# Linear attention and a gated expert layer on one core: q's clamp, the gates and the slots' tags on GpSimd, and the first pick ahead of q's phi

## The chip, the cores and the metric

The kernel runs on one core of a Trainium2 chip. A core has TensorE (PE in the profile; its weight loads are PEld), VectorE (DVE), ScalarE (ACT), GpSimd (POOL) and SyncE (SP), each with an instruction queue that it works through in order, and 16 DMA engines that the queues of SP, ACT and POOL feed. The metric is the time of one execution in device microseconds (us), the median of several runs.

## The reference

Eight batches of 576 tokens. First a linear attention over 8 heads of width 64, then for each token one expert out of 8, with a locality rule: the first token takes the expert of its largest logit, a later token takes its own only if its local gate is below one half, and else it keeps the expert of the token before it.

```python
def phi(x):
    return np.where(x > 0, x, np.exp(x) - 1.0) + 1.0
q_p, k_p = (phi(q), phi(k))
kv = np.einsum('bhsd,bhse->bhde', k_p, v)
z = np.sum(k_p, axis=2)
num = np.einsum('bhsd,bhde->bhse', q_p, kv)
den = np.einsum('bhsd,bhd->bhs', q_p, z)[..., None] + 1e-06
x = num / den                       # then (8, 576, 512), heads side by side
...
logits = np.einsum('bsd,de->bse', x, w_gate)
local_gate = 1.0 / (1.0 + np.exp(-np.einsum('bsd,de->bse', x, w_local).squeeze(-1)))
...
            if s == 0 or local_gate[b, s] < 0.5:
                e = fresh_e
            else:
                e = prev_e if prev_e >= 0 else fresh_e
...
            p = np.exp(ls)
            p /= p.sum() + 1e-09
            h = np.maximum(x[b, s] @ w1[e], 0.0)
            out[b, s] = p[e] * (h @ w2[e])
```

Everything is float32; `w1` is 8 x 512 x 1024 and `w2` 8 x 1024 x 512.

## The kernel before

**The bet.** The kernel assumes that in each batch every token ends with the expert of token 0. It computes that expert's output for the whole batch, and beside it a table `bad` that counts the tokens for which the assumption fails (a local gate below one half and another best expert). At the end the count is summed, and only if it is above 0 does a slow general program run (line 697).

**Stages of a batch `a`.** q, k and v come in two halves of four heads (`n = 2a + j`), each load 576 KB on SP's queue into a few fixed slots (4 for k, 2 for q, 3 for v). For each half:

- `E`: ScalarE takes the exponential of k or q (L229); for k, and for the four q halves of the batches 0 and 1 (`both`), it also writes relu in place (L231).
- `P` (`phi`): VectorE combines the two. Where relu is there, one instruction, `min(e, 1) + r` (L238, L246). Where it is not, that is for q from half 4 on, two: `max(r + 1, 1)` in place (L248, the clamp), then `min(e, that)` (L249).
- `VC`: GpSimd (for half 1 ScalarE) copies v beside a column of ones (L257). `K`: TensorE multiplies k and v over the tokens (L266); `KC` copies the result out of psum.
- `Q`, `QL`: TensorE transposes q (L277, L290), ScalarE copies it out (`QC`, `QLC`). The last 64 tokens, token 0 among them, go separately and early: `QL`, `NL` (numerators), `DL` (division, L303 to L306), `XL` (transpose of x, L364), `XLC` (copy to `xT`, L368), `R 0` (logits of these tokens, L379), `RC 0`.
- `N`, `D`, `X`, `XC`, `R 1`: the same for the other 512 tokens (L318, L306, L352, L357, L385).
- `PK` (`pick`): VectorE finds token 0's expert, and whether one of three weight slots in SBUF holds it already. `BK` (`book`) then writes the slots' `tag` and `age` (L418 to L424).
- `W`: GpSimd issues the DMA of w1 and w2 (float32 in memory, bf16 in SBUF), for batch 0 straight into `wcur`, later into a slot and only on a miss (L444, L446). Ahead of the later ones stands a tiny copy, `seen` (L438), that waits for the weights of the batch before. `CW` (`use`): VectorE copies a slot into `wcur` (L456).
- `SB`, `SBC`: the expert's number is spread over 128 partitions.
- The gate: `S1` (VectorE: maximum and difference, L476, L478), `S2` (ScalarE: exponential, L481), `S3` (VectorE, fourteen instructions L486 to L509: which token differs, the count `bad`, the sum and the gate value `pr`).
- `H`, `HC`: hidden layer, eight tiles on TensorE (L517), relu on ScalarE (L524). `O`, `OC`: output, five tiles (L534, L538), scaled by `pr` on ScalarE (L548, L550). `ST`: the stores on SP.

**What sets the order.** The order on every engine is fixed by hand, by a small list planner (`in_order`): each step has an engine, an assumed length, a rank (the lower goes first) and a list of steps that it needs; the planner plays this through and emits the steps in the order of their start. `WL` is a step that stands for the landing of weights; it exists only in the planner. The waits on the chip come from the tiles: an instruction waits for the writers and readers of what it touches. So a need that isn't a touch of the same tile changes an order, and adds no wait. Attention runs two batches (`LEAD = 2`) ahead of the expert layer; psum has two buffers for attention (`a`) and two for the expert layer (`m`).

Of the kernel before, what the change touches and what calls it, by code (L numbers as in the profile page):

```python
# [79 lines left out]
def kernel(  # L80
# [11 lines left out]
    nc = tc.nc  # L92
# [31 lines left out]
    bad = keep.tile([P, B], F32, name="bad")  # L124
    flag_i = keep.tile([1, 1], I32, name="flag_i")

    with ExitStack() as main:
# [105 lines left out]
        def phi(n, x, both=False, c0=0, c1=C):  # L233
# [10 lines left out]
            if both:  # L244
                for g in range(2):
                    nc.vector.scalar_tensor_tensor(e[:, g], e[:, g], 1.0, r[:, g], Alu.min, Alu.add)  # L246
            else:
                nc.vector.tensor_scalar(r, r, 1.0, 1.0, Alu.add, Alu.max)  # L248
                nc.vector.tensor_tensor(e, e, r, op=Alu.min)  # L249

# [162 lines left out]
        def book(b):  # L413
# [4 lines left out]
            nc.vector.tensor_copy(sf, si[:, 0:1])  # L418
            at = sm_.tile([1, E], F32, name="at")
            nc.vector.tensor_scalar(at, iof[0:1], sf, None, Alu.is_equal)  # L420
            for row, to in ((tag, e0f), (age, 0.01 * (b + 1))):
                dif = sm_.tile([1, E], F32, name="dif")
                nc.vector.scalar_tensor_tensor(dif, row, to, at, Alu.subtract, Alu.mult)
                nc.vector.tensor_tensor(row, row, dif, op=Alu.subtract)  # L424
# [48 lines left out]
        def soft(b):  # L473
            lt = lt_all[:, b]
            mx = st[b, "mx"] = gp.tile([P, NC], F32, name="mx")
            nc.vector.tensor_reduce(mx, lt[:, :, :E], axis=AX.X, op=Alu.max)  # L476
            ex = st[b, "ex"] = gp.tile([P, NC, E], F32, name="ex")
            nc.vector.tensor_tensor(ex, lt[:, :, :E], bc(mx), op=Alu.subtract)  # L478

        def soft_exp(b):  # L480
            nc.scalar.activation(st[b, "ex"], st[b, "ex"], Act.Exp)  # L481

        def gates(b):
            lt, mx, ex, e0b = lt_all[:, b], st[b, "mx"], st[b, "ex"], st[b, "e0b"]
            oh = sm_.tile([P, NC, E], F32, name="oh")
            nc.vector.tensor_tensor(oh, lt[:, :, :E], bc(mx), op=Alu.is_equal)  # L486
            sel = sm_.tile([P, 2, E], F32, name="sel")
            nc.vector.tensor_scalar(sel[:, 0, :], iof, e0b, None, Alu.is_equal)
            nc.vector.tensor_scalar(sel[:, 1, :], iof, e0b, 0.5, Alu.is_equal, Alu.subtract)

            def selb(i):
                return sel[:, i:i + 1, :].to_broadcast([P, NC, E])

            nc.vector.tensor_tensor(oh, oh, selb(1), op=Alu.mult)
            sc = sm_.tile([P, NC], F32, name="sc")
            nc.vector.tensor_reduce(sc, oh, axis=AX.X, op=Alu.add)
            fr = sm_.tile([P, NC], F32, name="fr")
            nc.vector.tensor_scalar(fr, lt[:, :, E], 0.0, None, Alu.is_lt)
            nc.vector.scalar_tensor_tensor(fr, sc, 0.5, fr, Alu.not_equal, Alu.mult)
            nc.vector.tensor_reduce(bad[:, b:b + 1], fr, axis=AX.X, op=Alu.add)  # L500
            ssum = sm_.tile([P, NC], F32, name="ssum")
            nc.vector.tensor_reduce(ssum, ex, axis=AX.X, op=Alu.add)
            nc.vector.tensor_scalar(ssum, ssum, 1e-9, None, Alu.add)
            rs = sm_.tile([P, NC], F32, name="rs")
            nc.vector.reciprocal(rs, ssum)
            nc.vector.tensor_tensor(ex, ex, selb(0), op=Alu.mult)
            pr = gp.tile([P, NC], F32, name="pr")
            nc.vector.tensor_reduce(pr, ex, axis=AX.X, op=Alu.add)
            nc.vector.tensor_tensor(pr, pr, rs, op=Alu.mult)  # L509
            gate[b] = pr  # L510
# [426 lines left out]
```

## Time and profile before

| | |
|---|---|
| median of 3 runs | 250.43 us (249.87 to 251.76) |
| the profiled execution | 250.41 us, its span 248.7 us |
| mean granted TensorE clock | 0.951 |
| DMA moved | 46.78 MB, mean 188 GB/s |

The span is the time from the first to the last instruction of the core; all rows of the trace are from this one execution. A row of a timeline has the start (us), the busy time, the engine, the line of the kernel, the operation, what it writes and reads, and in brackets how long the engine stood idle before and what released it. A row of the groups of lines has count, busy us, mean ns of one, and the idle time ahead of them. In the chain of waits each step has start, length, and the engine or DMA that held the end.

### The profile page before, as it was taken

The page shows a single profiled execution, that of the slowest core. Times are in us where ns is not written, and L with a number is a line of the kernel's source. Part 1 is how long each engine was busy: PE and PEld are TensorE (multiplying, and loading weights), DVE is VectorE, ACT ScalarE, POOL GpSimd, SP SyncE. Part 2 cuts the span into 40 slices and gives each one's busy share as a digit, 9 for nine tenths or more (in the row PEclk, how much of TensorE's full clock was granted, in tenths as well). Part 3 has the DMA queues.
Part 4 walks back from the last instruction along what each step waited for, and adds up shares of the span by engine and source line. Part 5 has one row for each costly group of instructions (what it writes and reads, how often), then busy time and mean ns, then how long its engine had stood idle before and what let it go on. Part 6 is the DMA issues. An engine that isn't in the chain of part 4 may idle for free.

```text
span 248.7 us, 8607 instructions
## 1 busy us (share of the span) xinstructions
PE 214.9 (86%) x3681; PEld 156.7 (63%) x3698; DVE 171.1 (69%) x496; ACT 146.7 (59%) x218; POOL 33.3 (13%) x54
## 2 busy tenths in 40 slices
PE   1255959999999999997999989999999999999960
PEld 0244847765777756784568755886578667747530
DVE  1756993989999999998996999979761676201000
ACT  4896762798585876824884893374235434646530
POOL 2123320200320131041001201312000011000000
PEclk9995575999999999999999999999999999999996
DMA  6998999960597088789983918990040049914023
GB/s 170 395 381 276 247 280 292 359 231 6 155 332 281 13 285 270 299 134 243 312 336 125 301 41 132 313 179 12 0 177 18 3 62 280 167 24 190 3 103 99
DMA packets 23532, 46.78 MB, mean 188 GB/s; under 512 B 3008, under 2 KB 8128, under 8 KB 22464
## 3 DMA queue, kind: packets, MB, share of 16 engines
q1 hardware_dynamic: 16160, 37.75, 43.0%
q0 software_dynamic: 6272, 8.39, 20.9%
q8 instruction: 31, 0.51, 0.8%
q10 hardware_dynamic: 1056, 0.02, 0.2%
q14 instruction: 13, 0.11, 0.1%
HBM read 61.88 MB, written 9.44 MB: 287 GB/s over the span
## 4 chain that ended last, share of the span: by engine, by line
PE 47%; DVE 32%; DMA 11%; issue 5%; ACT 1%; SPq 0%; DVEq 0%; POOLq 0%
PE hps L517 18%; PE yps L534 13%; DMA w1cur<-in_moe_w_dram 6%; PE kvps L266 5%; DVE xb L306 4%; DVE fq L249 4%; DMA qraw<-in_q_dram 3%; PE tq L277 3%; DVE kraw L238 2%; PE nps L318 2%; DVE qraw L248 2%; DVE w1cur L456 2%; PE yps L538 2%; DMA kraw<-in_k_dram 2%; DVE rec L305 2%
## 5 line engine op out<-in xcount | busy, mean ns | idle before, releaser
L517 PE MATMUL hps<-xT,w1cur 128*128 128x288 bf16 x512 | 70.4, 289 | 3.2 <-DMA w1cur<-in_moe_w_dram 3.0
L524 ACT ACTIVATE hT<-hps 128x576 bf16<-128x576 f32 x64 | 41.4, 657 | 35.3 <-PE hps L517 35.3
L534 PE MATMUL yps<-w2cur,hT 128*128 128x512 bf16 x239 | 57.7, 379 | 1.4 <-issue 0.8
L517 PEld LDWEIGHTS <-w1cur 128*128 128x128 bf16 x512 | 48.2, 98 | 15.9 <-DMA w1cur<-in_moe_w_dram 3.1
L548 ACT ACTIVATE yo<-yps,pr 128x512 f32<-128x512 f32 x32 | 22.0, 687 | 35.6 <-PE yps L534 35.6
L534 PEld LDWEIGHTS <-hT 128*128 128x128 bf16 x256 | 23.6, 98 | 25.1
L257 POOL COPY vone<-vraw 128x1152 f32<-128x1152 f32 x15 | 21.2, 1412 | 65.8 <-PE kvps L266 52.4
L266 PE MATMUL kvps<-vone,kraw 64*64 64x65 f32 x1152 | 23.2, 239 | 5.1 <-DVE wg L682 5.1
L266 PEld LDWEIGHTS kvps<-vone,kraw 64*64 64x64 f32 x1152 | 21.1, 152 | 8.3 <-POOL vone L257 5.4
L318 PE MATMUL nps<-kv,qT 64*64 64x65 f32 x1024 | 23.2, 234 | 2.0 <-issue 1.6
L318 PEld LDWEIGHTS nps<-kv,qT 64*64 64x64 f32 x1024 | 19.4, 145 | 6.5 <-issue 3.6
L306 DVE TENSOR_TENSOR xb<-nps,rec 128x512 bf16<-128x512 f32 x32 | 22.1, 692 | 1.1
L277 PE MATMUL tq<-ident,fq 128*128 128x128 f32 x128 | 19.1, 298 | 3.3 <-DVE fq L246 2.0
L238 DVE SCALAR_TENSOR_TENSOR kraw<-ek,kraw 128x1152 f32<-128x1152 f32 x15 | 21.9, 1465 | 0.0
L229 ACT ACTIVATE ek<-kraw 128x1152 f32<-128x1152 f32 x16 | 18.6, 1161 | 5.2 <-DMA kraw<-in_k_dram 3.9
L283 ACT COPY qT<-tq 128x512 f32<-128x512 f32 x32 | 18.5, 642 | 5.1 <-PE tq L277 5.1
L229 ACT ACTIVATE fq<-qraw 128x1152 f32<-128x1152 f32 (+2 forms) x18 | 19.2, 1066 | 1.5 <-DMA qraw<-in_q_dram 1.5
L277 PEld LDWEIGHTS tq<-ident,fq 128*128 128x128 f32 x128 | 16.1, 153 | 4.5 <-ACT kraw L231 2.1
L231 ACT ACTIVATE kraw<-kraw 128x1152 f32<-128x1152 f32 x15 | 17.5, 1164 | 0.5
L249 DVE TENSOR_TENSOR fq<-fq,qraw 128x1152 f32<-128x1152 f32 x12 | 17.1, 1427 | 0.4
L357 DVE COPY xT<-tx 128x1024 bf16<-128x1024 bf16 x16 | 10.9, 682 | 4.0 <-PE tx L352 4.0
L456 DVE COPY w2cur<-w2s 128x4096 bf16 x7 | 8.6, 1224 | 7.4 <-PE yps L538 7.3
(96 smaller groups left out, 205.2 us busy)
## 6 DMA issues: line engine op xcount, KB each, us to landing
kraw<-in_k_dram SPq DMA_DIRECT2D x16, 576.0 KB, 6.4
vraw<-in_v_dram SPq DMA_DIRECT2D x16, 576.0 KB, 8.7
out_dram<-yo SPq DMA_DIRECT2D x16, 512.0 KB, 4.8
qraw<-in_q_dram SPq DMA_DIRECT2D x14, 576.0 KB, 5.8
w1s<-in_moe_w_dram POOLq DMA_DIRECT2D x7, 1024.0 KB, 8.6
w2s<-in_moe_w_dram POOLq DMA_DIRECT2D x7, 1024.0 KB, 13.9
qraw<-in_q_dram SPq DMA_DIRECT2D x2, 512.0 KB, 8.5
w1cur<-in_moe_w_dram POOLq DMA_DIRECT2D x1, 1024.0 KB
```

The costliest lines, as they stand in the source:

```text
L229: nc.scalar.activation(e[:, :, c0:c1, :], raw_, Act.Exp)
L238: nc.vector.scalar_tensor_tensor(r, e, 1.0, r, Alu.min, Alu.add)
L249: nc.vector.tensor_tensor(e, e, r, op=Alu.min)
L257: nc.gpsimd.tensor_copy(vone[n % 2][:, :, :, :Dh], vraw[n % NV])
L266: nc.tensor.matmul(ps[g * PH:(g + 1) * PH, t, :W], lhsT=f[h, g, c, :], rhs=vo[h, g, c, :], start=(c == 0), stop=(c == C - 1))
L277: nc.tensor.transpose(ps[:, r, i * P:(i + 1) * P], ex_[n, "q"][:, 1 + i + (NC - 1) * r, :, :], identity=ident)
L306: nc.vector.tensor_tensor(dst, ps[:, :, :, :Dh], rec.rearrange("p g (m o) -> p g m o", o=1).to_broadcast([P, 2, m, Dh]), op=Alu.mult)
L318: nc.tensor.matmul(ps[o * PH:(o + 1) * PH, g, (il * 2 + t) * W:(il * 2 + t + 1) * W], lhsT=qT[n][g * PH:(g + 1) * PH, t, i * P + o * PH:i ...
L517: nc.tensor.matmul(ps[:, u, :HS], lhsT=w1b[:, kk, m * P:(m + 1) * P], rhs=xT[b][:, kk, u * HS:(u + 1) * HS], start=(kk == 0), stop=(kk == ...
L524: nc.scalar.activation(hT[b][:, m, :].rearrange("p (u s) -> p u s", u=2), open_.pop(("H", b, m))[:, :, :HS], Act.Relu)
L534: nc.tensor.matmul(ps[:, 0, :], lhsT=hT[b][:, m, i * P:(i + 1) * P], rhs=w2b[:, m, :], start=(m == 0), stop=(m == FK - 1))
L548: nc.scalar.activation(ym[:, i, :], ps[:, 0, :], Act.Copy, scale=pr[:, i:i + 1])
```

## The change

**q's clamp.** For q from half 4 on, `max(r + 1, 1)` moves from VectorE's `phi` to a new step `CL` on GpSimd, between `E` and `P`, for which `P` waits.

**The gate.** `S1` to `S3` become six steps: VectorE the maximum, GpSimd the difference and the comparison with 0, ScalarE the exponential, GpSimd the two selections and two products into one tile of three blocks, VectorE one sum over the three blocks with the small addend and the reciprocal, GpSimd the product and the test of the tokens. `bad` is kept per token group (40 columns in place of 8), so its sum per batch falls away and the last sum is over 40 columns.

**The tags.** `book` goes to GpSimd, with a subtraction and a product in place of each combined instruction.

**The order at the start.** Both halves of q's `phi` of batch 0, and all `phi` of batch 1, wait in the planner for `PK 0` (before, half 0 of q waited for `DL 0` only). The cast of the gate weights `wg` goes behind `KC 0` in place of behind an early `phi`. The loads of half 4 and later need `WL 0 0` in the planner. Some assumed lengths and ranks are changed.

```diff
-    bad = keep.tile([P, B], F32, name="bad")
+    bad = keep.tile([P, B, NC], F32, name="bad")
...
             else:
-                nc.vector.tensor_scalar(r, r, 1.0, 1.0, Alu.add, Alu.max)
                 nc.vector.tensor_tensor(e, e, r, op=Alu.min)
+
+        def clamp(n):
+            r = slot(n, "q").rearrange("p g c d -> p (g c d)")
+            nc.gpsimd.tensor_scalar(r, r, 1.0, 1.0, Alu.add, Alu.max)
...
-            nc.vector.tensor_copy(sf, si[:, 0:1])
+            nc.gpsimd.tensor_copy(sf, si[:, 0:1])
             at = sm_.tile([1, E], F32, name="at")
-            nc.vector.tensor_scalar(at, iof[0:1], sf, None, Alu.is_equal)
+            nc.gpsimd.tensor_scalar(at, iof[0:1], sf, None, Alu.is_equal)
             for row, to in ((tag, e0f), (age, 0.01 * (b + 1))):
                 dif = sm_.tile([1, E], F32, name="dif")
-                nc.vector.scalar_tensor_tensor(dif, row, to, at, Alu.subtract, Alu.mult)
-                nc.vector.tensor_tensor(row, row, dif, op=Alu.subtract)
+                nc.gpsimd.tensor_scalar(dif, row, to, None, Alu.subtract)
+                nc.gpsimd.tensor_tensor(dif, dif, at, op=Alu.mult)
+                nc.gpsimd.tensor_tensor(row, row, dif, op=Alu.subtract)
...
+        def gate_max(b):
+            mx = st[b, "mx"] = gp.tile([P, NC], F32, name="mx")
+            nc.vector.tensor_reduce(mx, lt_all[:, b, :, :E], axis=AX.X, op=Alu.max)
+
+        def gate_sub(b):
+            t3 = st[b, "t3"] = gp.tile([P, 3, NC, E], F32, name="t3")
+            nc.gpsimd.tensor_tensor(t3[:, 0], lt_all[:, b, :, :E], bc(st[b, "mx"]), op=Alu.subtract)
+            nc.gpsimd.tensor_scalar(t3[:, 2], t3[:, 0], 0.0, None, Alu.is_equal)
+
+        def gate_exp(b):
+            nc.scalar.activation(st[b, "t3"][:, 0], st[b, "t3"][:, 0], Act.Exp)
+
+        def gate_mul(b):
+            t3, e0b = st[b, "t3"], st[b, "e0b"]
+            sel = gp.tile([P, 2, E], F32, name="sel")
+            nc.gpsimd.tensor_scalar(sel[:, 0, :], iof, e0b, None, Alu.is_equal)
+            nc.gpsimd.tensor_scalar(sel[:, 1, :], iof, e0b, 0.5, Alu.is_equal, Alu.subtract)
+            for src, i, dst in ((2, 1, 2), (0, 0, 1)):
+                nc.gpsimd.tensor_tensor(t3[:, dst], t3[:, src],
+                                        sel[:, i:i + 1, :].to_broadcast([P, NC, E]), op=Alu.mult)
+
+        def gate_sum(b):
+            s3 = st[b, "s3"] = gp.tile([P, 3, NC], F32, name="s3")
+            nc.vector.tensor_reduce(s3, st[b, "t3"], axis=AX.X, op=Alu.add)
+            nc.vector.tensor_scalar(s3[:, 0], s3[:, 0], 1e-9, None, Alu.add)
+            nc.vector.reciprocal(s3[:, 0], s3[:, 0])
+
+        def gate_end(b):
+            s3 = st[b, "s3"]
+            pr = gate[b] = gp.tile([P, NC], F32, name="pr")
+            nc.gpsimd.tensor_tensor(pr, s3[:, 1], s3[:, 0], op=Alu.mult)
+            fr = bad[:, b, :]
+            nc.gpsimd.tensor_scalar(fr, lt_all[:, b, :, E], 0.0, None, Alu.is_lt)
+            nc.gpsimd.tensor_scalar(s3[:, 2], s3[:, 2], 0.5, None, Alu.is_lt)
+            nc.gpsimd.tensor_tensor(fr, fr, s3[:, 2], op=Alu.mult)
...
-                op(("Lk", n), "SP", 1.6, first, [n >= NKR and ("K", n - NKR)], lambda n=n: load_k(n))
+                op(("Lk", n), "SP", 1.6, first, [n >= NKR and ("K", n - NKR), n >= LEAD * NJ and ("WL", 0, 0)], lambda n=n: load_k(n))
...
-                    op(("P", x, n), "DVE", 1.36 if both else 2.15, r - 2 + (x == "q"),
-                       [("E", x, n), c0 and ("P0", n), c0 and (("PK", 0) if n else ("DL", 0)),
-                        0 < a < LEAD and ("PK", 0)],
+                    if x == "q" and not both:
+                        op(("CL", n), "POOL", 1.4, r - 3, [("E", x, n)], lambda n=n: clamp(n))
+                    op(("P", x, n), "DVE", 2.15 if x == "k" and not both else 1.36,
+                       r - 2 + (x == "q"),
+                       [("E", x, n), c0 and ("P0", n), (c0 or 0 < a < LEAD) and ("PK", 0),
+                        x == "q" and not both and ("CL", n)],
...
-            op(("BK", a), "DVE", 0.9, at + 8, [("PK", a)], lambda a=a: book(a))
+            op(("BK", a), "POOL", 1.2, at + 8, [("PK", a)], lambda a=a: book(a))
...
-                op(("CW", a, x), "DVE", 1.4, a * NU - 20,
+                op(("CW", a, x), "DVE", 1.2, a * NU - 20,
...
-            op(("S1", a), "DVE", 0.4, at + NU, [("RC", a, 0), ("RC", a, 1)], lambda a=a: soft(a))
-            op(("S2", a), "ACT", 0.25, at + NU, [("S1", a)], lambda a=a: soft_exp(a))
-            op(("S3", a), "DVE", 2.0, at + NU + 5, [("S2", a), ("SBC", a)],
-               lambda a=a: gates(a))
+            gr = at + NU
+            op(("S1", a), "DVE", 0.2, gr, [("RC", a, 0), ("RC", a, 1)], lambda a=a: gate_max(a))
+            op(("S2", a), "POOL", 0.4, gr, [("S1", a)], lambda a=a: gate_sub(a))
+            op(("S3", a), "ACT", 0.25, gr, [("S2", a)], lambda a=a: gate_exp(a))
+            op(("S4", a), "POOL", 0.8, gr + 1, [("S3", a), ("SBC", a)], lambda a=a: gate_mul(a))
+            op(("S5", a), "DVE", 0.65, gr + 2, [("S4", a)], lambda a=a: gate_sum(a))
+            op(("S6", a), "POOL", 0.7, gr + 2, [("S5", a)], lambda a=a: gate_end(a))
...
-        op(("WG",), "DVE", 0.3, -40, [("lat", "wg"), ("P0", 1)],
+        op(("WG",), "DVE", 0.3, -40, [("lat", "wg"), ("KC", 0)],
```

The loads of v and q get the same new need as those of k, and the outputs' copy (`OC`) now waits for `S6`.

More of the change, by code (lines that the diff above doesn't have):

```diff
@@ L483, in gates @@
[L483 to L510, printed above, removed]
@@ L582 @@
                 first = 3 * n if n >= NJ else n
[L583 to L584 removed]
+                op(("Lk", n), "SP", 1.6, first, [n >= NKR and ("K", n - NKR), n >= LEAD * NJ and ("WL", 0, 0)], lambda n=n: load_k(n))
+                op(("Lv", n), "SP", 1.6, first + 1 + (n < NJ), [n >= NV and ("VC", n - NV), n >= LEAD * NJ and ("WL", 0, 0)],
                    lambda n=n: load_v(n))
[L586 removed]
+                op(("Lq", n), "SP", 1.6, first + 2 + 2 * (n < NJ), [n >= NQR and ("P", "q", n - NQR), n >= LEAD * NJ and ("WL", 0, 0)],
                    lambda n=n: load_q(n))
@@ L674 @@
                    lambda a=a, i=i: output(a, i), takes="m")
-                op(("OC", a, i), "ACT", 0.7, a * NU + FK + i - 14, [("O", a, i), ("S3", a)],
+                op(("OC", a, i), "ACT", 0.7, a * NU + FK + i - 14, [("O", a, i), ("S6", a)],
                    lambda a=a, i=i: output_out(a, i), gives=("O", a, i))
@@ L687 @@
                 run[name]()
-        tot = bank2(ps_a, "tot", "a")[0:1, 0, :B]
-        nc.tensor.matmul(tot, lhsT=ones[:, 0:1], rhs=bad, start=True, stop=True)
+        tot = bank2(ps_a, "tot", "a")[0:1, 0, :B * NC]
+        nc.tensor.matmul(tot, lhsT=ones[:, 0:1], rhs=bad.rearrange("p b c -> p (b c)"), start=True, stop=True)
         fl = sm_.tile([1, 1], F32, name="fl")
```

9 lines of the change are left out of this document (removed).

## The prediction

> **What bounds the kernel now.** I read the page first, then the chain of waits, then busy times by stretch, then the timelines of single engines at the places where the chain turns.
>
> ```profile
> span 248.7 us, 8607 instructions
> PE 214.9 (86%) x3681; PEld 156.7 (63%) x3698; DVE 171.1 (69%) x496; ACT 146.7 (59%) x218; POOL 33.3 (13%) x54
> ```
>
> TensorE is busy for 214.9 of 248.7 us, so the whole of its idle time, 33.8 us, is more than any edit here can win. The chain of waits shows where the largest part of it lies:
>
> ```profile
> 22.85 14.81 DMA w1cur<-in_moe_w_dram
> 37.70 2.10 PE hps L517 x8
> ```
>
> The first expert layer cannot begin until batch 0's w1 has landed: 14.81 us from its issue at 22.85. After 37.70 the chain runs through VectorE for most of the middle of the run and through TensorE in its last part. The busy times of three stretches (span, length, then busy time and instructions of PE, PEld, DVE, ACT, POOL, then granted clock, DMA share, GB/s) say how much that is worth:
>
> ```profile
> 22.85:37.70 14.85, 9.85 (x232) 8.26 (x224) 13.42 (x30) 11.20 (x11) 5.58 (x4) 0.61 1.06 282
> 37.70:43.50 5.80, 5.79 (x88) 4.83 (x88) 1.73 (x11) 0.88 (x3) 0.00 (x0) 0.51 1.13 292
> 48.00:157.00 109.00, 103.07 (x1994) 75.11 (x1999) 100.52 (x289) 75.51 (x110) 15.63 (x22) 1.00 0.70 210
> ```
>
> Before 37.70 the DMA engines are saturated (1.06) and TensorE works at a granted clock of 0.61. From 37.70 it never rests, so what brings the first expert layer forward brings all that follows forward. From 48 to 157 VectorE is busy for 100.52 of 109 us (92%), but TensorE has only 109 - 103.07 = 5.93 us of gaps there. That is the most that relief for VectorE can win, however much work leaves it.
>
> ```profile
> PE nps L318 <- issue: 1.6, 1, 1.6
> PE lps L379 <- DVE xT L368: 1.1, 2, 0.8
> ```
>
> These are the two largest of those gaps in the list of waits: one is a single wait for psum space, the other waits for VectorE's copy of x.
>
> **The first pick.** The pick of batch 0 decides when w1 is asked for. VectorE and TensorE, in two timelines:
>
> ```profile
> 16.67 2.23 DVE L246 SCALAR_TENSOR_TENSOR fq<-fq,qraw 128x512 f32<-128x512 f32 x2
> 18.82 0.28 DVE L368 COPY xT<-txl 128x256 bf16<-128x256 bf16 x1
> ```
> ```profile
> 16.81 0.28 PE L364 MATMUL txl<-identb,xb 128*128 128x128 bf16 x2 [0.94 <-DVE xb L306]
> 19.05 1.48 PE L277 MATMUL tq<-ident,fq 128*128 128x128 f32 x8 [1.95 <-DVE fq L246]
> 20.46 0.39 PE L379 MATMUL lps<-wg,xT 128*64 128x9 bf16 x8
> ```
>
> The transposes end at 16.81 + 0.28 = 17.09, but the copy of x waits for q's phi until 18.82, and the logits then wait behind q's transposes until 20.46. With both phis of q held until after the pick, the copy can start at about 17.1 and the logits at 17.5. From their end to the issue of w1 it takes 22.85 - 20.85 = 2.00 us before, and nothing in those steps changes: w1 is issued at about 17.5 + 0.4 + 2.0 = 19.9, some 2.9 us earlier. The moved cast of wg has no part in this: it goes into the time in which VectorE waits for TensorE's first kv products. What pays is q's phi 0, which now runs after the pick, so its transposes and the first numerator of batch 0 come later, by up to the 1.48 + 0.4 us that they stood ahead of the logits.
>
> **The loads held back.** The hold is a rule of the order only: no load of the later batches reads or writes anything of w1, so the SP queue gets no wait on it. What the rule does is put the loads of k and v of batch 2 behind q's loads of batch 1:
>
> ```profile
> 18.96 0.37 SPq L145 DMA_DIRECT2D qraw<-in_q_dram  x1
> 19.42 0.42 SPq L145 DMA_DIRECT2D kraw<-in_k_dram  x1
> 19.89 0.46 SPq L145 DMA_DIRECT2D vraw<-in_v_dram  x1
> 23.27 0.37 SPq L145 DMA_DIRECT2D qraw<-in_q_dram  x1
> ```
>
> The two in the middle move behind the fourth, which waits for q's phi 1: from 19.4 to about 23, where they meet w1 in the engines instead of going ahead of it. The queue's shares in the window 22.85 to 37.7 (packets, MB, share of 16 engines) price that:
>
> ```profile
> q1 hardware_dynamic: 1309, 2.84, 56.9%
> q0 software_dynamic: 791, 1.32, 48.6%
> ```
> ```profile
> w1s<-in_moe_w_dram POOLq DMA_DIRECT2D x7, 1024.0 KB, 8.6
> ```
>
> Both queues are full there and halve the engines: 1.32 MB of weights cost 0.486 x 14.85 = 7.2 us of all sixteen, so w1's 1.05 MB is 5.7 us of work that takes twice as long beside loads. The later loads of the same size land in 8.6 us (median). So the bounds of w1's time are 8.6 (hold works as named) and 14.8 (it does nothing). I take 13.8, near the upper end, because q's loads and then k's and v's follow within 3 us, and only the first microsecond or so is without company: w1 lands at 19.9 + 13.8 = 33.7, and 28.5 at the best. The second condition of the first expert layer is x of batch 0:
>
> ```profile
> 32.80 0.69 DVE L357 COPY xT<-tx 128x1024 bf16<-128x1024 bf16 x1 [0.53 <-PE tx L352]
> ```
>
> That ends at 33.49 and, with phi 0 later by up to 1.9 but VectorE less busy with the pick, may fall between 32 and 35. So the layer starts at about 34.5 (32.0 to 36.5) in place of 37.7: **-3.2 us** (-5.7 to -1.2). Loads of batch 2 that come late are covered by the distance to their first use:
>
> ```profile
> 62.35 1.28 PE L266 MATMUL kvps<-vone,kraw 64*64 64x65 f32 x72
> ```
>
> That is some 40 us after their issue. q's first load of batch 2 can now stand ahead of a v load in SP's queue and hold it until q's slot is free, which has the same cover; without it, each late load would cost TensorE its own delay.
>
> **VectorE's relief.** The clamp of q, in the group of lines 48 to 157; then, from two timelines, the book of slots, and one gate:
>
> ```profile
> L248 DVE TENSOR_SCALAR qraw<-qraw 128x1152 f32<-128x1152 f32 x10 | 7.5, 749 | 0.0
> ...
> 58.60 0.13 DVE L418 CAST sf<-si 1x1 f32<-1x1 uint32 x1
> ...
> 59.53 0.15 DVE L424 TENSOR_TENSOR age<-age,dif 1x8 f32<-1x8 f32 x1
> ...
> 89.10 0.18 DVE L486 TENSOR_TENSOR oh<-lt_all,mx 128x40 f32<-128x40 f32 x1
> ...
> 91.38 0.17 DVE L509 TENSOR_TENSOR pr<-pr,rs 128x5 f32<-128x5 f32 x1
> ```
>
> Ten clamps are 7.5 us. A book is 59.68 - 58.60 = 1.08 us, five in the stretch, 5.4. The fourteen instructions of a gate take 91.55 - 89.10 = 2.45; three stay (one sum over three blocks, an add, a reciprocal), about 0.65, and the subtraction ahead of them goes (some 0.2): 2.0 saved, four times, 8.0. Together 20.9 us leave VectorE: 79.6 of 109 busy, 73%. TensorE's 5.93 us of gaps then remain where the wait is one of delay (logits behind a copy, a transpose behind a division), and close where VectorE was late because of its queue. I take 60%: **-3.5 us** (-5.9 to 0).
>
> **What GpSimd adds.** Nothing of before shows a clamp there. The nearest row is its copy of the same 128x1152 block; beside it VectorE's phi of k (ns: least, median, most):
>
> ```profile
> L257 POOL COPY vone<-vraw x15: 1146/1154/2316, 9.4 to 165.8; 128x1152 f32<-128x1152 f32 x15
> ...
> L238 DVE SCALAR_TENSOR_TENSOR kraw<-ek,kraw x15: 1336/1348/2233, 10.5 to 163.8; 128x1152 f32<-128x1152 f32 x15
> ```
>
> So a clamp is 1.15 to 2.32 us; I take 1.2, the median's neighbour, for one input and one output. Gap on gap, GpSimd has 109 - 15.63 = 93 us free. But the maxima show a price: the copy doubles and phi of k grows by 0.88 where the two meet. The Trainium skill ("SBUF — State Buffer", section "Who interferes with whom") says why: a VectorE instruction with two SBUF inputs and a GpSimd instruction that reads SBUF exclude each other for the whole of one. The trace agrees with it (2.32 and 2.23 us), and by it this change moves work onto the engine that locks VectorE out.
>
> A second price is the order on GpSimd itself. Its queue stands where a weight load waits for its slot, and the gate's three visits now stand in the same queue:
>
> ```profile
> 157.87 0.20 DVE L478 TENSOR_TENSOR ex<-lt_all,mx 128x40 f32<-128x40 f32 x1
> 157.99 0.75 DVE L248 TENSOR_SCALAR qraw<-qraw 128x1152 f32<-128x1152 f32 x1
> 158.15 1.07 POOL L446 DMA_DIRECT2D w2s<-in_moe_w_dram  x1 [8.25 <-DVE ex L478]
> ```
>
> Here GpSimd had stood for 8.25 us; a subtraction queued behind would start at 159.2, not 157.9, and ScalarE's exponential (with the evictions of hidden and output behind it), then VectorE's sum, would stand 1.3 us or more. In the other batches the weights were issued some us before the gate began, so I take one such stop in full: **+1.0 us** (0 to 10). The clamp ahead of phi costs q's path nothing: 1.2 in place of 0.75, and ScalarE's exponential is mostly long done. The wider total (40 sums for 8) lies beside the last stores.
>
> **Sum.** The profiled execution took 250.41 us (span 248.7 and 1.71 around it), the median of the runs is 250.43. 250.4 - 3.2 - 3.5 + 1.0 = **244.7**.
>
> **Rivals.**
> A, the forecast: 241 to 247.9, chance 0.47.
> B, all goes well: w1 alone in the engines lands in 8.6, x of batch 0 binds at 32.0, all gaps close, no stops: 250.4 - 5.7 - 5.9 = 238.8. For it: 5.93 us of gaps beside a VectorE at 92%. Against: the hold is not a wait. 0.07.
> C, the lock: each of the ten clamps costs a phi 0.88, 8.8 us, so VectorE is back at 88.4 of 109 (81%), and half of the 3.5 is lost with another 0.3 in the divisions behind: 246.7. For it, the maxima above; against, the medians, which show that most of the fifteen copies met nobody. 0.09. It is what the skill's rule gives, worked out from rows.
> D, no change: phi 0, put behind the pick, delays the first numerators by its 1.9 us, x of batch 0 is ready only at 36.5, gaps shrink by 1.0, stops cost 1.0: 250.4 - 1.2 - 1.0 + 1.0 = 249.2. For it, the transposes that ran at 19.05 ahead of the logits. 0.15.
> E, slower: GpSimd's queue becomes the wait. Each gate crosses it three times, in order behind copies (1.15), clamps (1.2) and weight issues (1.07); at about 1 us each on ScalarE's and VectorE's queues in seven batches, with half of it covered by TensorE's two psum buffers, that is 10 us: 250.4 - 6.7 + 10 = 253.7. It decides from 6.7 / 7, about 1 us lost by TensorE per batch. For it, the 8.25 us stand; against, GpSimd at 16 of 109 us busy and gates that have a whole batch of time. 0.22.
>
> A measurement of this kernel tells 1% (2.5 us) from no change. Below 247.9 lie A, B, C: faster 0.63; D, same 0.15; E, slower 0.22. The range leaves out the lower half of B and the upper part of E: 239.5 to 253.
>
> **What would show it.** Issue of w1 at about 20 and the first expert matmul at 32 to 36 (right), or 37 and later (D). Busy time of VectorE near 80 us in a like stretch, and TensorE's gaps there under 3 us. Waits of ScalarE's exponential or of VectorE's sum for GpSimd that add up to over 5 us would show E, phis of k or q over 2 us in most batches C. The forecast is wrong if TensorE's gaps after its first expert layer grow.

## The result and the profile after

The changed kernel takes 283.48 us (median of 4 runs, 279.28 to 284.22), beside 250.15 us for the kernel before: a ratio of 1.1235, 95% interval 1.1068 to 1.1403. The ratio rests on undisturbed runs alone and so lies a little below the quotient of the medians; the profiled execution took 283.80 us. It is slower by 12%, where 2% faster was forecast.

The first line of the page of after and its busy times:

```profile
span 282.0 us, 8626 instructions
PE 227.4 (81%) x3682; PEld 163.7 (58%) x3698; DVE 157.0 (56%) x346; ACT 146.1 (52%) x218; POOL 124.4 (44%) x202
```

VectorE is down from 171.1 to 157.0 us and GpSimd up from 33.3 to 124.4. TensorE's idle time, which was 33.8 us, is now 54.6. The middle of the run, by busy times in the stretch that the prediction used (columns as there):

```profile
48.00:157.00 109.00, 86.64 (x1470) 61.68 (x1476) 82.19 (x154) 57.08 (x83) 72.84 (x92) 0.89 0.60 177
```

TensorE's gaps in these 109 us (109 - 86.64) are 22.36 us, before 5.93, and the granted clock is 0.89, before 1.00. VectorE is busy for 82.19 us, close to the 79.6 forecast, but the stretch now holds fewer instructions of every engine but GpSimd: VectorE isn't relieved, it works on less.

From the chain that set the end, in order of time (start, length, what), GpSimd's pieces and one of VectorE's:

```profile
64.85 1.32 POOL t L485
66.26 1.31 POOL t L486
67.57 4.08 POOL qraw L252
...
103.01 3.77 DVE s L503
...
117.10 4.11 POOL qraw L252
...
147.33 4.02 POOL qraw L252
...
166.80 4.09 POOL qraw L252
...
180.60 4.03 POOL qraw L252
...
198.52 4.09 POOL qraw L252
```

GpSimd had no share of the chain before. Now its clamp of q (L252) stands on it six times, each time for 4.0 to 4.1 us. All twelve clamps are alike (ns: least, median, most; the start of the first and the last; shape):

```profile
L252 POOL TENSOR_SCALAR qraw<-qraw x12: 4091/4102/4112, 46.7 to 198.5; 128x1152 f32<-128x1152 f32 x12
```

The prediction took 1.2 us for it. The other piece to look at is `s` at L503, an addition of 1e-9 to 128x5 numbers that holds the chain for 3.77 us. What happens there is seen in a timeline of all engines, at another clamp (start, busy, engine, and in brackets the idle time before and who ended it):

```profile
73.18 0.77 DVE L503 TENSOR_SCALAR s<-s 128x5 f32<-128x5 f32 x1
...
73.89 4.10 POOL L252 TENSOR_SCALAR qraw<-qraw 128x1152 f32<-128x1152 f32 x1
...
74.08 4.77 DVE L248 TENSOR_TENSOR fq<-fq,qraw 128x1152 f32<-128x1152 f32 x1
...
78.78 0.28 DVE L371 COPY xT<-txl 128x256 bf16<-128x256 bf16 x1
...
79.11 0.39 PE L382 MATMUL lps<-wg,xT 128*64 128x9 bf16 x8 [5.86 <-DVE xT L371]
```

While GpSimd clamps one block of q (73.89 to 77.99), VectorE's phi of the other block takes 4.77 us instead of 1.36, the copy of x behind it in VectorE's queue waits, and TensorE stands for 5.86 us. In the whole run the largest phi of k is 3.84 us, of q 4.77, the largest weight copy 4.52. The product that takes one input from psum is never held, and neither is the reciprocal. From the page's groups (count, busy us, mean ns, idle before) and from the rows of one line (ns: least, median, most):

```profile
L238 DVE SCALAR_TENSOR_TENSOR kraw<-ek,kraw 128x1152 f32<-128x1152 f32 x15 | 26.8, 1792 | 0.5 <-ACT kraw L231 0.5
L248 DVE TENSOR_TENSOR fq<-fq,qraw 128x1152 f32<-128x1152 f32 x12 | 19.8, 1647 | 11.9 <-POOL qraw L252 11.7
```
```profile
L309 DVE TENSOR_TENSOR xb<-nps,rec x32: 691/691/693, 26.6 to 236.6; 128x512 bf16<-128x512 f32 x32
```
```profile
L308 DVE RECIPROCAL rec<-den x40: 178/203/205, 16.3 to 236.3; 128x8 f32<-128x8 f32 x32, 128x4 f32<-128x4 f32 x8
```

### The profile page after: what moved, and what is told of

It reads as the page before. It is cut to its first block, busy times and chain, and to the rows that moved or that the text cites. A ratio compares the mean times of both kernels' runs of the same rounds, so it can differ in the third digit from the quotient of the medians.

```text
span 282.0 us, 8626 instructions
## 1 busy us (share of the span) xinstructions
PE 227.4 (81%) x3682; PEld 163.7 (58%) x3698; DVE 157.0 (56%) x346; ACT 146.1 (52%) x218; POOL 124.4 (44%) x202
## 4 chain that ended last, share of the span: by engine, by line
PE 47%; DVE 20%; POOL 16%; issue 11%; DMA 2%; SPq 1%; DVEq 0%; POOLq 0%
PE hps L521 18%; PE yps L538 10%; POOL qraw L252 9%; PE kvps L269 6%; DVE kraw L238 4%; PE nps L321 4%; PE tq L280 2%; DVE xb L309 2%; DMA vraw<-in_v_dram 2%; DVE s L503 2%; POOL vone L260 2%; DVE fq L248 2%; PE tx L355 2%; PE yps L542 1%; DVE w1cur L460 1%
## 5 line engine op out<-in xcount | busy, mean ns | idle before, releaser
L521 PE MATMUL hps<-xT,w1cur 128*128 128x288 bf16 x512 | 73.9, 297 | 0.0
L538 PE MATMUL yps<-w2cur,hT 128*128 128x512 bf16 x240 | 59.8, 390 | 1.9 <-issue 1.4
L252 POOL TENSOR_SCALAR qraw<-qraw 128x1152 f32<-128x1152 f32 x12 | 49.2, 4101 | 0.0
L260 POOL COPY vone<-vraw 128x1152 f32<-128x1152 f32 x15 | 19.4, 1295 | 28.9 <-DMA vraw<-in_v_dram 16.8
L321 PE MATMUL nps<-kv,qT 64*64 64x65 f32 x1024 | 25.8, 249 | 6.3 <-DVE den L306 2.7
L321 PEld LDWEIGHTS nps<-kv,qT 64*64 64x64 f32 x1024 | 21.6, 158 | 11.4 <-issue 5.1
L238 DVE SCALAR_TENSOR_TENSOR kraw<-ek,kraw 128x1152 f32<-128x1152 f32 x15 | 26.8, 1792 | 0.5 <-ACT kraw L231 0.5
L248 DVE TENSOR_TENSOR fq<-fq,qraw 128x1152 f32<-128x1152 f32 x12 | 19.8, 1647 | 11.9 <-POOL qraw L252 11.7
L309 DVE TENSOR_TENSOR xb<-nps,rec 128x512 bf16<-128x512 f32 x32 | 22.1, 692 | 1.1
L274 DVE COPY kv<-kvps 128x130 f32<-128x130 f32 x16 | 4.7, 291 | 31.5 <-PE kvps L269 31.5
L450 POOL DMA_DIRECT2D w1s<-in_moe_w_dram x7 | 2.8, 398 | 38.8 <-DVE rec L308 21.9
```

Of the source, the lines that this page charges most:

```text
L238: nc.vector.scalar_tensor_tensor(r, e, 1.0, r, Alu.min, Alu.add)
L252: nc.gpsimd.tensor_scalar(r, r, 1.0, 1.0, Alu.add, Alu.max)
L260: nc.gpsimd.tensor_copy(vone[n % 2][:, :, :, :Dh], vraw[n % NV])
L309: nc.vector.tensor_tensor(dst, ps[:, :, :, :Dh], rec.rearrange("p g (m o) -> p g m o", o=1).to_broadcast([P, 2, m, Dh]), op=Alu.mult)
L321: nc.tensor.matmul(ps[o * PH:(o + 1) * PH, g, (il * 2 + t) * W:(il * 2 + t + 1) * W], lhsT=qT[n][g * PH:(g + 1) * PH, t, i * P + o * PH:i ...
L521: nc.tensor.matmul(ps[:, u, :HS], lhsT=w1b[:, kk, m * P:(m + 1) * P], rhs=xT[b][:, kk, u * HS:(u + 1) * HS], start=(kk == 0), stop=(kk == ...
```

## The experiments

Diffs are against the kernel named in the heading. "Before" ran beside each; intervals are of the ratio to it.

**The whole change, the clamp back on VectorE (e1).**

```diff
-        nc.gpsimd.tensor_scalar(r, r, 1.0, 1.0, Alu.add, Alu.max)
+        nc.vector.tensor_scalar(r, r, 1.0, 1.0, Alu.add, Alu.max)
```

> The whole change except that q's clamp is on VectorE again, as before. Theory (the clamp, 4.1 us on GpSimd where 1.2 was assumed, is the loss): 242 to 248 us, VectorE's phi of k back to about 1.5 us in the mean, and GpSimd busy for about 75 us. Rival (the gate and the tags that cross GpSimd's queue are the loss): above 262, with ScalarE's exponential and VectorE's sum still waiting for GpSimd for over 5 us in total.

251.21 us, 1.0094 (1.005 to 1.0138), far below the rival's 262 and yet above the 242 to 248 that were expected. The clamp carries 1.1235 - 1.0094 = 11.4% of before, 28.5 of the 31 us lost. The rest (new start, gates, tags and the changed lengths in the planner) wins nothing in sum.

**Before, with the clamp alone on GpSimd (e2).** The same line moved the other way.

> The kernel before with q's clamp alone moved to GpSimd. Theory: most of the loss is here, 270 to 290 us. Rival (gates and tags): 250 to 258, because without them little else waits for GpSimd.

287.54 us, 1.1543 (1.1473 to 1.1612). The clamp alone does all of the damage. Its groups on VectorE (count, busy us, mean ns, idle before):

```profile
L459 DVE COPY w2cur<-w2s 128x4096 bf16 x7 | 15.7, 2236 | 8.7 <-PE yps L541 8.7
L423 DVE TENSOR_SCALAR at<-iof,sf 1x8 f32<-1x8 f32 x7 | 13.2, 1883 | 0.2
```
```profile
L423 DVE TENSOR_SCALAR at<-iof,sf x7: 218/360/4497, 63.5 to 241.7; 1x8 f32<-1x8 f32 x7
```

The comparison of 8 numbers has a mean of 1.88 us and a maximum of 4.50: no size protects from the price. The kind of instruction does. Among the held are the phis, with two inputs in SBUF, the copies of weights, and small additions and comparisons (`tensor_scalar` from SBUF to SBUF). Products from psum and reciprocals kept their lengths, as the rows of L309 and L308 above show for the change.

**The whole change, the planner told 4.1 us for the clamp (e3).**

```diff
-    op(("CL", n), "POOL", 1.4, r - 3, ...
+    op(("CL", n), "POOL", 4.1, r - 3, ...
```

> The whole change, with the planner told 4.1 us for the clamp in place of 1.4, so that the order allows for it. Theory (the clamp's time on the shared port and on GpSimd's queue): 266 to 282 us, since the blocked time of VectorE stays. Rival (the order, made for a clamp of 1.4 us, is the loss): 246 to 257.

272.85 us, 1.0959 (1.0891 to 1.1027). By the ratios 6.9 us of the loss (1.1235 - 1.0959) came from an order made for a clamp of 1.4 us; the two intervals lie close together, so the size is rough. Most of the loss stays.

**One operation in place of two on GpSimd (e4).** GpSimd takes `max(r, 0)` and VectorE the combined instruction that the `both` halves use.

```diff
-    nc.gpsimd.tensor_scalar(r, r, 1.0, 1.0, Alu.add, Alu.max)
+    nc.gpsimd.tensor_scalar(r, r, 0.0, None, Alu.max)
```

> The whole change, with GpSimd doing one operation, max(r, 0), and VectorE the rest in the combined form that it uses for the first batches. If the clamp's time goes by the number of its operations it takes 2.0 to 2.6 us here and the kernel 252 to 268; if one operation runs like the copy it takes 1.2 us and the kernel 243 to 250; if the time belongs to the kind of instruction it stays at 4.1 us and the kernel at 276 to 285.

271.63 us, 1.0861 (1.0749 to 1.0974).

```profile
L252 POOL TENSOR_SCALAR qraw<-qraw 128x1152 f32<-128x1152 f32 x12 | 37.4, 3115 | 0.0
```

No expectation had 3.1 us, or this time. With one operation it is 3.12, with two 4.10, beside a copy of the same block at 1.15: on this block GpSimd's price goes by the number of operations, and a copy is no measure for it.

**An idle clamp (e5): e1, and GpSimd does an instruction like the clamp whose result nobody uses.** The real clamp stays on VectorE.

```diff
+    src = ident.rearrange("p (o c) -> p o c", o=1).to_broadcast([P, C, P])
+    nc.gpsimd.tensor_scalar(scr, src, 1.0, 1.0, Alu.add, Alu.max)
```

> The run with the clamp back on VectorE (251.2 us), plus an operation on GpSimd of the clamp's size and kind at the clamp's old place, that reads a constant and writes a scratch tile: nobody waits for its result. If the loss comes by the shared port and by GpSimd's queue (not by phi waiting for the clamp), 265 to 285 us, with single instructions of VectorE stretched to 3 us and more. If it comes by phi waiting for the clamp's result, 251 to 257.

283.65 us, 1.133 (1.1221 to 1.1439): the whole loss, with nobody waiting for the clamp. Two rows of its timeline, GpSimd's and VectorE's:

```profile
106.96 4.10 POOL L260 TENSOR_SCALAR scr<-ident 128x1152 bf16<-128x1152 f32 x1
...
107.33 3.75 DVE L511 TENSOR_SCALAR s<-s 128x5 f32<-128x5 f32 x1
```

The clamp ends at 111.06, the 5 numbers at 111.08. The two share no data. VectorE's instruction began beside GpSimd's and was held to its end.

**Idle memsets (e6): four short instructions that write scratch and read nothing, in place of the idle clamp.**

```diff
+    for _ in range(4):
+        nc.gpsimd.memset(scr, 0.0)
```

> The same with four memsets of the scratch tile in place of that operation: they occupy GpSimd's queue but read nothing from SBUF. If the queue alone makes the loss, as long as for the run before in proportion to the time that the memsets take; if the port does, 251 to 256 us, with VectorE's phi of k back at 1.5 us in the mean.

261.98 us, 1.0478 (1.0398 to 1.0559), between the two expectations, GpSimd as busy as in e5 (134.3 and 133.6 us). So some 10 us over e1 (1.0478 - 1.0094) come with any such work in GpSimd's queue, 21 more (1.133 - 1.0478) from something that the clamp has and the memsets haven't: it reads, and it is one long instruction. VectorE's busy time shows where these 21 us arise: 151.1 us in e1, 155.2 in e6, 181.7 in e5. The next two runs tell reading and length apart.

**The idle clamp in four pieces (e13).**

```diff
+    for i in range(4):
+        d = scr[:, 2 * i:2 * i + 2, :]
+        src = ident.rearrange("p (o c) -> p o c", o=1).to_broadcast([P, 2, P])
+        nc.gpsimd.tensor_scalar(d, src, 1.0, 1.0, Alu.add, Alu.max)
```

> The idle clamp of the earlier run, cut into four instructions of 256 elements a partition each (1024 of 1152 elements in all), which read the identity and write scratch, each with two operations; nobody waits for their result, and the clamp that computes stays on VectorE. Theory 1 (what VectorE pays is that GpSimd reads SBUF, for as long as it reads, and the cut does not matter): phi of k has a mean near the 1940 ns of the uncut one, its largest above 3 us, and the time is 278 to 284 us. Theory 2 (what VectorE pays is the length of a single GpSimd instruction: between short ones it gets its turn): no VectorE instruction is held by more than about one piece (some 1 us), phi of k falls to a mean of 1.5 to 1.65 us with its largest near 2.3, and the time is near the 262 us of the memsets. Both expect GpSimd busy for 125 to 135 us, as with the uncut one.

261.25 us, 1.0454 (1.0407 to 1.05), with GpSimd at 142.5 us and VectorE back at 149.6. Reading in short instructions costs what the memsets cost. What is left are waits of the gate for GpSimd. The sum on VectorE and the exponential on ScalarE, first in e1, then in e13 (us in all, times, longest):

```profile
DVE s L503 <- POOL t L498: 9.0, 6, 2.5
...
ACT t L490 <- POOL t L487: 2.7, 3, 1.9
```
```profile
DVE s L512 <- POOL t L507: 25.2, 7, 7.0
...
ACT t L499 <- POOL t L496: 17.8, 6, 5.7
```

The gate's instructions stand in GpSimd's queue behind the pieces, and what waits for them waits longer.

**One long memset (e16)**, 3.08 us at the median.

```diff
+    scr = keep.tile([P, 28, P], mybir.dt.uint8, name="scr")
...
+    nc.gpsimd.memset(scr, 0)
```

> The idle memsets of the earlier run as one long memset per block of q (128x3584 one-byte elements, at the rate of the two-byte memset some 3.2 us; were it much faster for the narrower type, under 2.5 us, the run would tell nothing). It reads nothing, and nobody waits for it. Theory 1 (any long GpSimd instruction keeps VectorE out): instructions of VectorE with maxima above 3 us as with the idle clamp, phi of k with a mean above 1.75 us, 273 to 282 us. Theory 2 (it must also read SBUF; a long one that only writes lets VectorE go on): phi of k stays at a mean of 1.4 to 1.6 us with its largest under 2.5, and the time is 256 to 262 us, the share of GpSimd's queue.

265.48 us, 1.0604 (1.0501 to 1.0707), above what was expected of harmless and below what was expected of harmful. VectorE's rows tell why. First the clamp and the phi of k in e16 (an execution of 270.14 us), then the same in e13 (ns: least, median, most):

```profile
L248 DVE TENSOR_SCALAR qraw<-qraw x12: 736/1851/3646, 46.4 to 186.8; 128x1152 f32<-128x1152 f32 x12
...
L238 DVE SCALAR_TENSOR_TENSOR kraw<-ek,kraw x15: 1342/1347/2291, 10.9 to 172.1; 128x1152 f32<-128x1152 f32 x15
```
```profile
L248 DVE TENSOR_SCALAR qraw<-qraw x12: 739/750/1009, 46.4 to 180.0; 128x1152 f32<-128x1152 f32 x12
...
L238 DVE SCALAR_TENSOR_TENSOR kraw<-ek,kraw x15: 1342/1348/2839, 10.8 to 166.1; 128x1152 f32<-128x1152 f32 x15
```

The long memset holds VectorE's clamp, with one input, for up to 3.65 us, but no phi of k, with two, for over 2.29, which before already reached beside a copy (2.23); the long reading clamp of e5 held both (maxima 4.55 and 4.71). The Trainium skill ("SBUF — State Buffer", section "Who interferes with whom") has this: the shared pair of ports is held for a whole instruction; VectorE's one-input copies and `tensor_scalar` in a two-port mode clash with any GpSimd instruction, two-input ones only with one that reads. These rows agree with it in who is held and by what; which mode VectorE used no row names. By e5 and e13 (1.133 - 1.0454) the price here is 22 us for twelve clamps.

**The change's own clamp in four pieces (e15)**, 288 elements each.

```diff
-    nc.gpsimd.tensor_scalar(r, r, 1.0, 1.0, Alu.add, Alu.max)
+    for i in range(4):
+        p = r[:, i * 288:(i + 1) * 288]
+        nc.gpsimd.tensor_scalar(p, p, 1.0, 1.0, Alu.add, Alu.max)
```

> The whole change with one edit: GpSimd's clamp of q is issued as four instructions of 288 elements a partition, each with both operations, in place of one of 1152. The work on GpSimd is the same or a little more (4.5 to 6 us per clamp with four starts). Theory 1 (VectorE is locked out for the length of a single GpSimd instruction, so short ones let it in between): most of the loss goes; phi of k falls from a mean of 1792 to 1.5 to 1.65 us, no 5-element instruction of VectorE takes over 2 us, and the time is 257 to 265 us: what remains is GpSimd's queue (some 10 us, by the short idle pieces) and q's phi, which waits for the last piece. Theory 2 (in the real change it is the wait of q's phi for a long clamp that costs, whatever its cut): the time stays at 278 to 286 us.

281.44 us, 1.1222 (1.1107 to 1.1338): nothing won, against what e13 had led to expect. The groups of VectorE:

```profile
L238 DVE SCALAR_TENSOR_TENSOR kraw<-ek,kraw 128x1152 f32<-128x1152 f32 x15 | 22.7, 1518 | 0.5 <-ACT kraw L231 0.5
...
L248 DVE TENSOR_TENSOR fq<-fq,qraw 128x1152 f32<-128x1152 f32 x12 | 17.3, 1440 | 25.5 <-POOL qraw L254 25.5
```

The lock is nearly gone (phi of k from 1792 to 1518 ns, phi of q from 1647 to 1440; in the kernel before they are 1465 and 1427), but now VectorE stands for 25.5 us at phi of q, waiting for the clamp. In the change that wait was 11.7 us, with VectorE busy for 157.0 us; here it is busy for 140.5. The time that was spent in held instructions is now spent in waiting. The planner had put phi of q some 1.4 us behind the clamp.

**The pieces, and the planner told 5.0 us (e17).**

```diff
-    op(("CL", n), "POOL", 1.4, r - 3, ...
+    op(("CL", n), "POOL", 5.0, r - 3, ...
```

> The whole change with the clamp in four pieces of 288 elements and the planner told 5.0 in place of 1.4 us for it, so that q's phi is ordered later behind it. Theory 1 (two prices that can each be paid alone: a long instruction locks VectorE out, and cut into pieces it makes q's phi wait at the head of VectorE's queue because the planner took it for short): VectorE's waits for q's clamp fall from 25.5 us to under 12, and the time is 258 to 268 us, near the idle pieces. Theory 2 (GpSimd's clamp cannot be had earlier, since its loads and exponential come just in time and its slots are few): the waits stay near 20 us and the time is 273 to 283 us.

261.93 us, 1.0475 (1.0372 to 1.0578). The wait falls to 10.0 us:

```profile
ACT t L491 <- POOL t L488: 16.7, 5, 4.8
...
DVE s L504 <- POOL t L499: 12.4, 7, 2.5
DVE fq L248 <- POOL qraw L254: 10.0, 5, 4.9
```

(Waiting engine and line, whom it waits for, us in all, times, longest.) The other two are the gate's waits for GpSimd. The sum's 12.4 us are little more than e1's 9.0, where no clamp is in that queue; the exponential's 16.7 us are far more than e1's 2.7. The four runs of the same clamp side by side, as ratios to before:

| | one instruction | four pieces |
|---|---|---|
| planner told 1.4 | 1.1235 (after) | 1.1222 (e15) |
| planner told 4.1 or 5.0 | 1.0959 (e3) | 1.0475 (e17) |

The pieces alone take back nothing that can be measured, the planner's length alone some 7 us, both together 19 (7.6% of before). A long clamp is paid either as a lock or as a wait at the head of VectorE's queue.

**The new start and the pieced clamp, gates and tags on VectorE (e18).**

> The kernel before with the new start, and of GpSimd's new work only the clamp of q, in four pieces of 288 elements, the planner told 5.0 us for it; gates and tags stay on VectorE and the weight copy's length stays at 1.4. If the queue of GpSimd costs because gates stand behind clamps in it, this is 247 to 255 us, as gates are not in it; if the clamp costs through q's phi wherever it runs on GpSimd, it is 258 to 275 us. Under 246 us only if relief of VectorE pays at all, which neither theory expects after the clamp on ScalarE.

254.18 us, 1.014 (1.0039 to 1.024); VectorE's wait for the clamp is 0.5 us, GpSimd busy for 94.6. Without gates and tags in GpSimd's queue 8 us of e17's 12 us over before go, though e17 also has the shorter planner length for a weight copy, priced further below. It is still 6.4 us slower than the start alone (1.014 - 0.9886, e7), with GpSimd's clamp as the only other change.

**The new start alone (e7): before, with the needs of the first pick, the loads and `wg`.**

```diff
-    [("E", x, n), c0 and ("P0", n), c0 and (("PK", 0) if n else ("DL", 0)), 0 < a < LEAD and ("PK", 0)],
+    [("E", x, n), c0 and ("P0", n), (c0 or 0 < a < LEAD) and ("PK", 0)],
...
-    [("lat", "wg"), ("P0", 1)],
+    [("lat", "wg"), ("KC", 0)],
```

> The kernel before with the order of the start alone (phi of q behind the first pick, later loads behind batch 0's weights, the cast moved). If the start's 3 us, which the run with the clamp back shows at the first expert layer, reach the end, 245 to 248 us here (the kernel before at 249 to 250). If the middle of the run gives them back, 249 to 251, with the first expert matmul at 35 us all the same.

247.28 us (12 runs), 0.9886 (0.9851 to 0.9921): the fastest of all, 2.9 us better than before.

**The start, and the clamp of q as relu on ScalarE (e10)**, which makes phi of q one instruction.

```diff
-BOTH = "k"
+BOTH = "kq"
```

> The order of the start as in the run with it alone, and q's clamp on ScalarE for all batches, as relu, so that VectorE has one combined instruction in place of two. If VectorE's relief is worth what was forecast for it, 242 to 247 us; if ScalarE, 12 x 1.16 us = 14 us busier, becomes the wait, 250 to 256.

249.34 us, 0.998 (0.9943 to 1.0016): 2.4 us worse than e7, with VectorE's 8 us less.

```profile
PE 213.5 (86%) x3682; PEld 155.8 (63%) x3698; DVE 162.3 (65%) x496; ACT 158.7 (64%) x230; POOL 30.8 (12%) x54
```

ScalarE has 12 us more, and the time lies between the two expectations, so the run doesn't say that relief is worth nothing, only that it isn't worth that.

**Gates or tags alone (e8, e9).** e8 is e1 with the gates back on VectorE, so it has start and tags; e9 is e1 with the tags back.

> The change with q's clamp and the gates on VectorE: the start and the tags on GpSimd remain. If the gates on GpSimd cost what the start wins, 245 to 248.5 us (the run with the clamp back alone took 251.2); if the tags do, 250 to 252.5.

> The change with q's clamp and the tags on VectorE: the start and the gates on GpSimd remain. If the tags on GpSimd cost what the start wins, 245 to 248.5 us; if the gates do, 250 to 252.5.

252.49 us, 1.013 (1.0079 to 1.0181), and 251.51 us, 1.0069 (1.0036 to 1.0102). Both are slower than e7, by 6.1 and 4.6 us, and e8 with almost nothing moved is the slower. By the expectations e8 would blame the tags and e9 the gates, and both can't carry the same loss. That pointed to what both share with the change and e7 doesn't: the planner's length for a weight copy.

**That length alone (e11 on e7, e14 on before; e12 takes it back from e1).**

```diff
-    op(("CW", a, x), "DVE", 1.4, a * NU - 20,
+    op(("CW", a, x), "DVE", 1.2, a * NU - 20,
```

> The order of the start alone, and the planner's length of the weight copies 1.2 in place of 1.4 us, as in the change. The runs with gates or tags back both stayed above 251 where the start alone gave 247.3. If that is this length (another order of the same work), 250 to 253; if it is what GpSimd does in those runs, 246 to 248.5.

> The kernel before with one number changed: the planner is told 1.2 in place of 1.4 us for a copy of weights, as the whole change does; no instruction is added, removed or put on another engine. Theory 1 (the number acts on its own, by the order that it makes): 1 to 2.5% slower, 252.5 to 256 us. Theory 2 (the number acts only on top of the new start, by chance of the order there): within 0.5% of before, 249 to 251.5 us.

> The change with q's clamp on VectorE and the length of the weight copies at 1.4 us again. If the length is what ate the start's gain, 244 to 248 us; if gates and tags on GpSimd ate it, 250 to 253.

e11: 252.47 us, 1.0123 (1.0057 to 1.0189), 5.9 us worse than e7. e14: 252.82 us, 1.0139 (1.0102 to 1.0176), 3.5 us worse than before. e12: 250.27 us, 1.0033 (0.9994 to 1.0071), 1.5 us better than e1. In these pairs only the order of the same instructions differs. So e8 and e9 can't price tags and gates: the order they fall into weighs as much. At the old length gates and tags together cost 1.0033 - 0.9886, 3.7 us (e12 against e7), and this too holds an order along with the work.

## Why the prediction was wrong

By the ratios, the steps of the change from before: start -2.9 us (e7), gates and tags +3.7 (e12), the weight copy's length +1.5 (e1), the clamp +28.5 (after). The planner's length had no term in the sum. Gates and tags had one stop of 1.0 us, and the clamp had nothing, at 1.2 us each.

**The step that failed** is "So a clamp is 1.15 to 2.32 us; I take 1.2, the median's neighbour, for one input and one output." It measured 4.10 us, outside both ends. The nearest row was taken, but a copy is no arithmetic: e4 shows 3.12 us with one operation. With it fell "The clamp ahead of phi costs q's path nothing": at this length the clamp isn't covered (11.7 us of waits in the change, 25.5 in e15). Whether 1.2 us would have been covered no run shows. The lock, which the prediction saw, stood in a rival alone; in the sum it was nothing.

**Rival C had the mechanism and not the size.** It priced a lock at 0.88 us, the difference of a median and a maximum beside a copy of 1.15 us. With clamps of 4.1 us single instructions of VectorE grew to 3.8 to 4.8 (after, e5): the price follows from the clamp's length. The rule of the Trainium skill ("SBUF — State Buffer", section "Who interferes with whom") had it, since by it the lock lasts for the whole of the other instruction. Rival C also counted phis alone; copies of weights and additions on 5 numbers were held as well. Shown by e5, e13 and e16 for the idle clamp: 22 us of lock at this length. How the 28.5 us of the change's own clamp split into lock, waits of phi and waits of the gate is not measured as neatly, since cutting it turns one into the other (e15).

**Rival E's mechanism** is there too, at some 9 to 10 us in e13 and e6 over e1, close to its 10. The closeness is luck: E counted clamps of 1.2 us, and these runs had 4.7 us (e6) and 5.8 us (e13) of work in the place of each. With no clamp in the queue gates and tags cost 3.7 us (e12), and here too the prediction's +1.0 for one stop was too low.

**The start was right.** Of after:

```profile
17.42 0.29 DVE L371 COPY xT<-txl 128x256 bf16<-128x256 bf16 x1 [0.49 <-PE txl L367]
...
20.20 0.99 POOL L448 DMA_DIRECT2D w1cur<-in_moe_w_dram  x1 [2.37 <-issue]
...
33.34 0.69 DVE L360 COPY xT<-tx 128x1024 bf16<-128x1024 bf16 x1 [0.53 <-PE tx L355]
...
34.59 0.56 PE L388 MATMUL lps<-wg,xT 128*128 128x9 bf16 x16
35.00 1.14 PE L521 MATMUL hps<-xT,w1cur 128*128 128x288 bf16 x8
```

Copy at 17.42 (forecast 17.1), issue of w1 at 20.20 (19.9), first expert layer at 35.00 (34.5); e7 gains 2.9 us of the 3.2. What binds the layer is no longer w1: before, TensorE stood 3.03 us for its landing, now it comes to the layer without a gap, straight from the logits, for which x was ready at 34.03. The same row of before:

```profile
37.70 2.10 PE L517 MATMUL hps<-xT,w1cur 128*128 128x288 bf16 x8 [3.03 <-DMA w1cur<-in_moe_w_dram]
```

So the forecast landing at 33.7 isn't seen in any wait; w1 was there by 35.00, at most 14.8 us after its issue. In e7's profiled run the layer starts later, and about half of the gain lies behind it:

```profile
36.27 1.14 PE L517 MATMUL hps<-xT,w1cur 128*128 128x288 bf16 x8
```

The held loads did no harm that shows in e7's time.

**VectorE's relief gave nothing.** e12 has gates and tags on GpSimd with the old length, and the clamp on VectorE. Its stretch:

```profile
48.00:157.00 109.00, 103.27 (x1946) 73.79 (x1944) 89.53 (x207) 74.13 (x109) 48.86 (x101) 0.98 0.73 217
```

VectorE falls from 100.52 to 89.53 us, and TensorE's gaps are 5.73 us after 5.93. The 60% were a choice without a row behind them: 11 us less on VectorE closed 0.2 us of gaps. They were not the same gaps. TensorE's waits in that stretch of e12:

```profile
PE hps L522 <- issue: 2.0, 1, 2.0
PE nps L322 <- DVE den L307: 1.3, 2, 0.7
...
PE lps L383 <- DVE xT L372: 0.2, 1, 0.2
```

The wait of the logits for the copy of x fell from 1.1 to 0.2 us, as hoped, but 2.0 us of `issue` ahead of the hidden layer and 1.3 us for a step of the division (`den`) stand in its place. The larger of the two gaps that the prediction showed was put down to psum space; its row says `issue`, which names no cause. e12 also has another order than before, so this is no clean price of relief. Whether all 20.9 us would do more, without a lock, was not tried by itself.

**The sign of failure.** The text named growing gaps after the first expert layer as the sign of its failure, and that is the sign that came: 22.36 us.

## What to carry to other kernels

Before moving work to GpSimd, find a row of the same operation there, with as many arithmetic steps; if there is none, a copy gives a floor and no estimate, and a longer instruction that reads also holds VectorE's copies and two-input instructions in SBUF for its whole length, small ones included. If it must move, cut it into pieces of about a microsecond and tell the planner what they take in sum; and ask first whether the engine to be relieved is late because it is full, or only because each step waits for another. A change that alters a planner's lengths must be tested with these alone, since another order of the same work moved this kernel by 1.4% (e14) and, on the new start, by 2.4% (e11 against e7).

## What the runs showed of the hardware

- GpSimd on 128x1152 float32: copy 1.15 us (before), `tensor_scalar` with one operation 3.12 (e4), with two 4.10 (after); a memset of as many bf16 elements 1.06 (e6).
- Single VectorE instructions on 5 or 8 numbers took up to 4.50 us beside one GpSimd clamp (e2); in e5 one of 3.75 us ended within 0.02 us of it (111.06 and 111.08).
- In the same runs VectorE's products from psum (at most 0.69 us) and reciprocals (at most 0.21) kept their length (after, L309 and L308).
- A long GpSimd memset held VectorE's one-input clamp (up to 3.65 us) and not its two-input phi of k (at most 2.29, e16).
- TensorE's granted clock was 0.89 in the stretch with 22.36 us of gaps (after) and 1.00 in that with 5.93 (before).
